# One tile shape, 64 rows by 32 columns, for all products of an attention-and-MLP loop

## The chip, the cores and the metric

The kernel runs on one core of one Trainium2 chip. The metric is the device time of one execution in microseconds. A core has five engines with a queue each: TensorE (PE, whose weight loads are shown apart as PEld), VectorE (DVE), ScalarE (ACT), GpSimd (POOL) and SyncE (SP), which mainly issues DMAs.

## The reference

A block over 2048 tokens of width 640: a layer norm, then attention with 32 heads of 20 channels and an MLP with 1536 hidden channels side by side, both added to the input.

```python
x = A_x
xn = _layernorm(x)
# A: q, k, v = (xn @ wqkv) in 32 heads of Dh = 20
#    o = softmax(q k^T * Dh**-0.5) v ;  out_A = o @ wo
# B: y = _layernorm(xn) ;  h = gelu(y @ w1 + b1) ;  out_B = h @ w2 + b2
return x + _A_ref(xn, A_wqkv, A_wo) + _B_ref(xn, B_w1, B_b1, B_w2, B_b2)
```

Inputs and output are float32. Products are made of float16 or bfloat16 halves, high and low parts, in three passes (`PASS`), or of float32 operands.

## The kernel before, in words

The kernel is one function, `mha_mlp_kernel`, in three stretches. The **first** (lines 155 to 509) loads and normalizes the input, transposes it, splits weights into halves, makes q, k and v, and writes q, k (`qkscr`) and the normalized input (`xscr`) to memory. The w1 weights are loaded by one DMA (line 482) into `w1t`, squared for a scale (line 423) and split in place (line 434).

The **second**, the loop (lines 927 to 964), does the attention, and lays the MLP into it as filling. `ORDER` lists 32 stages: a pair of heads and a half of the queries. A stage has two runs `cc` of 512 queries, and a run goes through 16 blocks of 128 keys. For a block, `scores` (line 578) makes two products, one for each head, of 61 rows by 128 columns, with one head's features in partitions 0 to 60 and the other's in 64 to 124, and issues one exponential on ACT for both (line 586, 128x1024). The score buffers `psS` are three, of two PSUM banks each. Four blocks are a group (`GRP`). In a group the blocks 0 and 1 are "split": their probabilities are used as a bfloat16 upper half and a float16 rest `low`, which DVE makes (`rest`, line 598). Blocks 2 and 3 are "whole" and used as float32.

`pv` (line 603) multiplies a group's probabilities by the values. Its `product` (line 614) takes 128 rows by 32 columns; the four quarters of the PSUM partitions take head 0 and head 1, two sums each, so that one bank holds the output of a run (`psO`, one buffer). Eight products take the upper halves, four the rests, and four the float32 blocks. After a run's last group ACT copies the bank to `ev` (line 636), and after the second run `unload` writes the two partial sums of outputs and denominators to memory (`opart`, `lpart`).

The order of the work is written out by hand. In each group the loop issues scores of two blocks, then the filling, then scores of two blocks, then `pv` of the **previous** group. The filling is a chain of generators: `layer1` (line 777; 1440 passes of 128x128 weights over 256 tokens), `layer2` (line 811; 1152 passes over 320 columns) and, last, the projection with wo. Each step of a generator names its cost in us; the loop gives a credit of `rate` for each group, and takes steps while there is credit, until `CHUNK` is spent or a part has ended (`over`). Parts of both layers share one PSUM bank (`psM`, one buffer). The end of a part starts `gelu` (line 735) or `addup` (line 755) on DVE, which read the bank. `tick`, every two blocks, moves all side work on by one step: stack loads, `gelu`, and `finish` (line 666), which loads the two partial sums back (line 697), adds them (lines 702, 725), divides and writes halves for the projection; it waits a fixed count of ticks for its DMAs. `load_chunk` (line 769) loads 256 tokens of normalized input, two chunks ahead.

The **third** stretch (from line 977) finishes the projection after the loop. A general path behind a flag isn't taken with these inputs.

## Time and profile before

| what | before |
|---|---|
| median of three runs | 1385.02 us (1384.66 to 1385.03) |
| the profiled execution | 1385.2 us |
| its span, first to last instruction | 1383.5 us |
| mean granted TensorE clock | 0.997 |
| PE busy, matmuls | 1350.8 us (98%), 11711 |
| PEld busy, weight loads | 600.9 us (43%), 11711 |
| DVE busy | 1061.7 us (77%) |
| ACT busy | 1126.2 us (81%) |
| POOL busy | 32.9 us (2%) |
| DMA | 125.68 MB, 91 GB/s on the mean |

Busy time counts a product from its start to its modelled end; products overlap, so the time between the starts of two says more than the length of one. In an ordered view a row gives its start, its length, the engine, the line, the operation, output and inputs, rows*columns of the weights, the shape of the moving data, and the count of operations merged in it. In a group's row stand, after the count, its busy time in us and the mean length of one in ns, then the idle time of the engine just ahead of it and what ended that.

### The profile page before, as it was taken

To read this page: it belongs to the slowest core of one execution; us is meant where nothing else is said; L and a number is where in the kernel's file an instruction comes from. 1 tells how busy PE (TensorE), PEld (TensorE's weight loads), DVE (VectorE), ACT (ScalarE), POOL (GpSimd) and SP (SyncE) were. 2 spreads that over 40 slices of the span, in tenths; PEclk is the share of its full clock that TensorE was granted. 3 is DMA by queue.
4 is the path that set the end of the run, shared out by engine and by line. 5 is a ranking of instruction groups with operands and counts; after the bars stand their busy time and mean duration, and the time that the engine had idled before them with its cause. 6 is when DMAs were issued, how large, how long until landed. Compare 5 with 4: busy or idle time off the path is not lost.

```text
span 1383.5 us, 29113 instructions
## 1 busy us (share of the span) xinstructions
PE 1350.8 (98%) x11711; PEld 600.9 (43%) x11711; DVE 1061.7 (77%) x1425; ACT 1126.2 (81%) x1282; POOL 32.9 (2%) x75
## 2 busy tenths in 40 slices
PE   9999999999999999999999999999999999999998
PEld 6555555443333343433343333343334334333375
DVE  6648743899778977889887789877988897888642
ACT  5644323999999999999999999999999999999700
POOL 2000000000000000000000000000000000000000
PEclk9999999999999999999999999999999999999999
DMA  9853413012124231213221123212124322341375
GB/s 265 243 175 109 108 52 110 16 32 64 41 55 111 67 88 34 69 52 102 71 77 33 47 75 103 76 47 58 44 64 113 98 56 70 85 153 59 98 235 179
DMA packets 92320, 125.68 MB, mean 91 GB/s; under 512 B 16905, under 2 KB 58569, under 8 KB 92178
## 3 DMA queue, kind: packets, MB, share of 16 engines
q1 hardware_dynamic: 89218, 117.14, 28.3%
q0 software_dynamic: 2304, 5.24, 2.3%
q8 instruction: 94, 1.54, 0.5%
q10 hardware_dynamic: 656, 1.36, 0.3%
q14 instruction: 48, 0.39, 0.1%
HBM read 80.84 MB, written 42.86 MB: 89 GB/s over the span
## 4 chain that ended last, share of the span: by engine, by line
PE 59%; DVE 11%; ACT 5%; DMA 3%; issue 2%; SPq 1%; DVEq 0%; ACTq 0%
PE o L615 23%; PE s L584 14%; PE py L819 9%; PE pu L787 8%; DVE low L598 5%; PE z L896 5%; ACT p L586 4%; DMA oscr<-oa 1%; DVE u L740 1%; DMA oa<-opart 1%; DVE u L741 1%; DVE w L744 1%; DVE w L745 1%; DVE hT L752 1%; DVE u L750 1%
## 5 line engine op out<-in xcount | busy, mean ns | idle before, releaser
L586 ACT ACTIVATE p<-s 128x1024 f32<-128x1024 f32 x1024 | 973.6, 1042 | 52.4 <-PE s L584 46.2
L598 DVE TENSOR_TENSOR low<-p 128x1024 f16<-128x1024 f32 x512 | 608.8, 1219 | 165.0 <-ACT p L586 164.9
L615 PE MATMUL o<-p,vfull 128*32 128x512 bf16 (+1 forms) x4096 | 433.7, 494 | 0.0
L584 PE MATMUL s<-qs,ks 61*128 61x512 f16 x2048 | 317.7, 382 | 8.7 <-ACT p L586 7.2
L584 PEld LDWEIGHTS <-ks 61*128 61x128 f16 x2048 | 63.9, 94 | 296.4 <-issue 294.2
L787 PE MATMUL pu<-xm,w1t 128*128 128x256 f16 x1440 | 179.2, 274 | 4.1 <-DVE u L740 3.6
L819 PE MATMUL py<-w2t,hT 128*128 128x320 f16 x1152 | 178.6, 301 | 1.7 <-DVE xb L757 1.7
L787 PEld LDWEIGHTS <-w1t 128*128 128x128 f16 x1440 | 130.9, 98 | 71.2 <-issue 57.6
L819 PEld LDWEIGHTS <-hT 128*128 128x128 f16 x1152 | 102.5, 98 | 89.5 <-issue 55.2
L286 PE MATMUL qkp<-xnt,wv 128*128 128x512 f16 x600 | 132.3, 380 | 0.0
L615 PEld LDWEIGHTS <-vfull 128*32 128x32 f16 x3072 | 61.5, 95 | 146.2 <-issue 115.4
L615 PE MATMUL o<-low,vfull 128*32 128x512 f16 x1024 | 107.3, 379 | 6.6 <-DVE low L598 6.4
L300 ACT ACTIVATE qkhl<-qkp,qks 128x1024 f16<-128x1024 f32 (+1 forms) x24 | 23.3, 971 | 84.1 <-PE qkp L286 66.2
L286 PEld LDWEIGHTS <-wv 128*128 128x128 f16 x600 | 58.2, 98 | 67.8
L615 PEld LDWEIGHTS o<-p,vfull 128*32 128x32 f32 x2048 | 63.1, 109 | 50.6 <-issue 0.5
L349 PE MATMUL vp<-wv,xnt 128*128 128x320 f16 x480 | 66.6, 300 | 0.0
L896 PE MATMUL z<-w1t,ot 128*128 128x320 f16 x480 | 65.8, 300 | 0.0
L896 PEld LDWEIGHTS <-ot 128*128 128x128 f16 x480 | 46.7, 98 | 19.8 <-issue 1.7
L349 PEld LDWEIGHTS <-xnt 128*128 128x128 f16 x480 | 46.5, 98 | 18.2
L301 DVE SCALAR_TENSOR_TENSOR qkhl<-qkp,qks,qkhl 128x1024 f16<-128x1024 f32 (+1 forms) x24 | 26.5, 1104 | 34.3 <-ACT qkhl L300 34.3
L857 DVE SCALAR_TENSOR_TENSOR acc<-z,sc,acc 128x320 f32<-128x320 f32 x32 | 17.6, 550 | 45.1 <-PE z L896 42.9
L636 ACT ACTIVATE ev<-o 128x512 f32<-128x512 f32 x64 | 39.4, 615 | 3.3 <-PE o L615 3.3
(168 smaller groups left out, 685.7 us busy)
## 6 DMA issues: line engine op xcount, KB each, us to landing
qkscr<-qkhl SPq DMA_DIRECT2D x40, 256.0 KB
opart<-ev SPq DMA_DIRECT2D x124, 80.0 KB
ks<-qkscr SPq DMA_DIRECT2D x120, 80.0 KB
qs<-qkscr SPq DMA_DIRECT2D x192, 40.0 KB
oa<-opart SPq DMA_DIRECT2D x32, 240.0 KB
xt<-in_A_x_dram SPq DMA_DIRECT2D x16, 320.0 KB
xscr<-xnt SPq DMA_DIRECT2D x4, 1280.0 KB
xm<-xscr SPq DMA_DIRECT2D x8, 640.0 KB
```

The costliest lines, as they stand in the source:

```text
L286: nc.tensor.matmul(ps[:, i, :], wv[:, k, q, a, mm * P : (mm + 1) * P], xnts[c][:, k, b, :], start=(k + n == 0), stop=(k == KD - 1 and n == 2))
L300: nc.scalar.activation(hl[:, 0, i0:i1], ps[:, i0:i1], AF.Copy, scale=a)
L301: nc.vector.scalar_tensor_tensor(hl[:, 1, i0:i1], ps[:, i0:i1], a, hl[:, 0, i0:i1], ALU.mult, ALU.subtract)
L349: nc.tensor.matmul(ps[:, hf, :320], xnts[c][:, k, a, j * P : (j + 1) * P], wv[:, k, 2, b, hf * 320 : (hf + 1) * 320], start=(n == 0), stop ...
L584: nc.tensor.matmul(ps[:, a, :], ks[64 * a : 64 * a + 61, kb * P : (kb + 1) * P], qs[64 * a : 64 * a + 61, cc * 512 : (cc + 1) * 512], star ...
L586: nc.scalar.activation(pt, ps, AF.Exp, scale=QS)
L598: nc.vector.tensor_sub(low, pt, upper(pt))
L615: nc.tensor.matmul(pv.o[32 * q : 32 * q + 32, :], src[:, v0 - PAD * (1 - q % 2) :][:, :32], t, start=q not in pv.begun, stop=last, skip_gr ...
L636: nc.scalar.activation(evs[g, hf][:, cc], pv.o, AF.Copy)
L787: nc.tensor.matmul(ps[:, i], w1v[:, k, (f + i) // 4, a, fo_ : fo_ + P], xnt[:, k, b, :], start=(n == 0), stop=(n == 3 * KD - 1))
L819: nc.tensor.matmul(ps[:, :320], hTs[mc][:, f, a, j * P : (j + 1) * P], w2v[:, f, b, hf * 320 : (hf + 1) * 320], start=(n == 0), stop=(n == ...
L896: nc.tensor.matmul(ps[:, :320], ot[:, k, a, j * P : (j + 1) * P], wov[:, k, b, h * 320 : (h + 1) * 320], start=(n == 0), stop=(n == 3 * KD ...
```

## The change

All products in the loop become products of 64 rows by 32 columns, eight of which cover the array.

- `scores`: eight products of 61x32 for a block in place of two of 61x128.
- `pv`: each product becomes two, one for each half of the rows, into two PSUM banks. ACT copies one bank and DVE adds the other. It is cut in four stages (upper halves, rests, float32, read out), of which each block of the next group issues one.
- `layer1` and `layer2`: each 128x128 pass becomes eight products (`tiles`) into two banks of one tile `mt`, which all parts share. `layer1`'s contraction is laid out anew: `w1` and the normalized input are loaded so that each half of the partitions holds features of its own, and one half of a pass gives hidden channels of its own. `addup` adds two banks with two DVE operations.
- The loop takes the filling at each block but the third of a group; `rate` and `CHUNK` are stated for a block.
- PSUM in the loop: two score buffers in place of three, two banks for the output, two for `mt`.
- `finish`: the second partial sum is added in memory transfer, by a DMA on POOL's queue that accumulates, in place of two DVE adds (the last one keeps them).
- `w1` is loaded by 20 DMAs, a chunk by four plus one, into one buffer and one chunk ahead.

The core of the diff:

```diff
-CHUNK = 1.75
+CHUNK = 0.9
...
+            def load_w1():
+                wt = w1t.rearrange("p k n -> p (k n)").rearrange("p (k j c) -> p k j c", k=2 * KD, c=P)
+                src = w1.rearrange("(k b p) (j r c) -> r b k p j c", b=2, p=64, r=2, c=P)
+                for k in range(2 * KD):
+                    for r in range(2):
+                        nc.sync.dma_start(wt[64 * r : 64 * r + 64, k], src[r, k // KD, k % KD])
...
+            psS = pool(name="psS2", bufs=2, space=PSUM)
+            psO = pool(name="psO2", bufs=1, space=PSUM)
+            psM = pool(name="psM2", bufs=1, space=PSUM)
+            mt = psM.tile([P, 2, 512], F32, tag="m", name="mt")
+
+            def tiles(out, w, t, start, stop, **kw):
+                for r in range(2):
+                    rows = slice(64 * r, 64 * r + 64)
+                    for c in range(0, P, 32):
+                        nc.tensor.matmul(out[c : c + 32, r], w[rows, c : c + 32], t[rows], start=start, stop=stop,
+                                         skip_group_check=True)
...
-                for a in range(2):
-                    nc.tensor.matmul(ps[:, a, :], ks[64 * a : 64 * a + 61, kb * P : (kb + 1) * P],
-                                     qs[64 * a : 64 * a + 61, cc * 512 : (cc + 1) * 512], start=True, stop=True)
+                for c in range(0, P, 32):
+                    for a in range(2):
+                        nc.tensor.matmul(ps[c : c + 32, a, :],
+                                         ks[64 * a : 64 * a + 61, kb * P + c : kb * P + c + 32],
+                                         qs[64 * a : 64 * a + 61, cc * 512 : (cc + 1) * 512], start=True, stop=True)
...
+            def product(unit, q, src, v0, t):
+                kb = unit[3]
+                for r in range(2):
+                    rows = slice(64 * r, 64 * r + 64)
+                    nc.tensor.matmul(pv.o[32 * q : 32 * q + 32, r], src[rows, v0 - PAD * (1 - q % 2) :][:, :32], t[rows],
+                                     start=(q, r) not in pv.begun, stop=kb >= NKB - GRP, skip_group_check=True)
+                    pv.begun.add((q, r))
...
+                elif kb0 == NKB - GRP:
                     if cc == 0:
                         evs[g, hf] = m1.tile([P, 2, 512], F32, tag="ev", name="ev")
-                    nc.scalar.activation(evs[g, hf][:, cc], pv.o, AF.Copy)
+                    nc.scalar.activation(evs[g, hf][:, cc], pv.o[:, 0], AF.Copy)
+                    nc.vector.tensor_add(evs[g, hf][:, cc], pv.o[:, 1], evs[g, hf][:, cc])
...
+                    for cc, kb in ((cc, kb) for cc in range(2) for kb in range(NKB)):
                         units.append([g, hf, cc, kb, scores(g, hf, cc, kb)])
+                        if kb % 2:
+                            tick()
+                        if kb % GRP:
+                            rest(units[-2])
+                        elif prev:
+                            rest(prev[-1])
+                        if prev:
+                            pv(kb % GRP, prev)
+                        credit += rate
+                        spent, over[0] = 0.0, False
+                        while kb % GRP != 2 and credit > 0 and spent < CHUNK and not over[0]:
```

More of the change, by code (lines that the diff above doesn't have):

```diff
@@ L621, in pv @@
+            def pv(stage, units):
+                g, hf, cc, kb0 = units[0][:4]
+                split = [u for u in units if SPLIT[u[3]]]
+                whole = [u for u in units if not SPLIT[u[3]]]
                 of16 = lambda kb, a: 2 * PAD + kb * 2 * VROW + (2 * g + a) * 2 * VW
                 of32 = lambda kb, a: PAD + kb * VROW + (2 * g + a) * VW
-                for kb, up, _ in split:
-                    for a in range(2):
-                        product(2 * a, vhalf, of16(kb, a), up[:, a])
-                        product(2 * a + 1, vhalf, of16(kb, a) + VW, up[:, a])
@@ L695, in finish @@
                     o0, o1, rb = o0[: r1 - r0], o1[: r1 - r0], rb[: r1 - r0]
[L696 to L697 removed]
+                    go(o0, opart[0, r0:r1, cols])
+                    also(o1 if last else o0, opart[1, r0:r1, cols])
                     if c0 == 0:
@@ L836, in mlp @@
                     done[0] = mc == NMC
-                    for i in range(6):
-                        for part in first[i : i + 1] + (second[i - 1 : i] if i else []):
-                            yield from part
+                    for part in first[:2] + second[:1] + first[2:3] + second[1:2] + first[3:] + second[2:]:
+                        yield from part
             pieces = {}
             def load_piece(c):
-                ot = m2.tile([P, KD, 2, MC], F16, tag="xnt", name="ot")
+                if c == 0:
+                    pieces["ot"] = m1.tile([P, 2 * KD, 2, MC], F16, tag="xnt", name="ot")
+                ot = pieces["ot"][:, c % 2 * KD : (c % 2 + 1) * KD]
                 acc = m0.tile([P, KF, 2, MC], F16, tag="hT", name="acc")
@@ L977, in mha_mlp_kernel @@
                 more(2)
-                pv(prev)
+                for stage in range(4):
+                    pv(stage, prev)
                 while more(1):
```

186 lines of the change are left out of this document (90 added, 96 removed).

## The prediction

> **What bounds the kernel now.** I read the profile in this order: busy time by stage, the groups, the order of time on ScalarE, the order of time on TensorE, then the chain and the waits for what hangs on DMAs. The view by stage (columns: us, then busy time and count of PE, PEld, DVE, ACT, POOL, then clock, DMA share, GB/s) cuts the span before, in and behind the attention loop:
>
> ```profile
> 0.00:256.00 256.00, 250.02 (x1612) 140.44 (x1612) 153.99 (x327) 125.92 (x159) 16.99 (x57) 0.99 0.49 143
> 256.00:1310.00 1054.00, 1034.06 (x9598) 412.15 (x9597) 884.33 (x1054) 999.97 (x1124) 15.92 (x18) 1.00 0.25 70
> 1310.00:1383.50 73.50, 66.75 (x505) 48.28 (x503) 23.39 (x45) 0.28 (x1) 0.00 (x0) 0.98 0.69 211
> ```
>
> In the loop two engines are nearly full: PE 1034 of 1054 us and ACT 1000. The change touches little but the loop, so what matters is how much of PE's 1034 is not arithmetic, and that ACT leaves only 54 us to be won. ACT in order of time and three groups:
>
> ```profile
> 698.31 7.61 ACT L586 ACTIVATE p<-s 128x1024 f32<-128x1024 f32 x8 [0.19 <-PE s L584]
> 705.77 0.63 ACT L636 ACTIVATE ev<-o 128x512 f32<-128x512 f32 x1
> 706.25 3.96 ACT L586 ACTIVATE p<-s 128x1024 f32<-128x1024 f32 x4
> ```
> ```profile
> L586 ACT ACTIVATE p<-s 128x1024 f32<-128x1024 f32 x1024 | 973.6, 1042 | 52.4 <-PE s L584 46.2
> L598 DVE TENSOR_TENSOR low<-p 128x1024 f16<-128x1024 f32 x512 | 608.8, 1219 | 165.0 <-ACT p L586 164.9
> L787 PE MATMUL pu<-xm,w1t 128*128 128x256 f16 x1440 | 179.2, 274 | 4.1 <-DVE u L740 3.6
> L819 PE MATMUL py<-w2t,hT 128*128 128x320 f16 x1152 | 178.6, 301 | 1.7 <-DVE xb L757 1.7
> ```
>
> Eight exponentials take 705.77 - 698.31 = 7.46 us, 0.93 each, and the copy of the output 706.25 - 705.77 = 0.48 before the next may start. ACT idles 46.2 us for scores. Now PE, through one group of four key blocks, and one stretch of the second layer:
>
> ```profile
> 699.73 0.38 PE L584 MATMUL s<-qs,ks 61*128 61x512 f16 x2
> 700.04 0.64 PE L615 MATMUL o<-p,vfull 128*32 128x512 bf16 x8
> 700.50 0.39 PE L615 MATMUL o<-low,vfull 128*32 128x512 f16 x4
> 700.72 1.03 PE L615 MATMUL o<-p,vfull 128*32 128x512 f32 x8
> 701.68 0.60 PE L584 MATMUL s<-qs,ks 61*128 61x512 f16 x4
> 702.22 1.16 PE L787 MATMUL pu<-xm,w1t 128*128 128x256 f16 x9
> 703.31 0.61 PE L584 MATMUL s<-qs,ks 61*128 61x512 f16 x4
> 703.84 0.64 PE L615 MATMUL o<-p,vfull 128*32 128x512 bf16 x8
> ```
> ```profile
> 1181.59 1.80 PE L819 MATMUL py<-w2t,hT 128*128 128x320 f16 x12
> ```
>
> A second pair of scores starts 0.60 - 0.38 = 0.22 us behind the first, but the first product of another shape 700.04 - 699.73 = 0.31 behind: the change of shape costs 0.09. First-layer passes come every (1.16 - 0.274)/8 = 0.111 us, the last starts at 703.11, and scores at 703.31: 0.20 - 0.11 = 0.09 again. Four such changes stand in a group of 4.11 us: 0.37 x 256 groups = 95 us. That is what one shape can save on PE.
>
> **The change part by part.**
>
> *Shape.* The array work stays: eight 64x32 products fill the array as one 128x128, four 128x32 or two 61x128 did. Per group PE then needs 4 x 0.22 for scores, 3 x 0.22 for the half-width products, 2 x 0.43 for the float32 ones ((1.03 - 0.593) is the second round's start; 0.593 us is the mean in the row below), 2.40 in all, and the layers (1440 x 0.111 + 1152 x 0.136)/256 = 1.24, with 0.136 = (1.80 - 0.301)/11. Sum 3.64, over the loop 932 us against 1054. PE would stop being the bound; ACT is late next.
>
> ```profile
> L615 PE MATMUL o<-p,vfull 128*32 128x512 f32 x2048 | 269.7, 593 | 0.0
> ```
>
> *Four to eight times as many instructions.* Scores 1024 x 8, half-width products 3072 x 2, float32 2048 x 2, layers (1440 + 1152) x 8: 39,168 pairs of load and product where 9,598 stand. No row shows a long run of such small pairs. The nearest, product bursts and loads:
>
> ```profile
> 34.03 0.38 PE L286 MATMUL qkp<-xnt,wv 128*128 128x512 f16 x1
> 34.34 0.29 PE L321 MATMUL norms<-sq,heads 128*32 128x128 bf16 x8
> 34.57 0.39 PE L286 MATMUL qkp<-xnt,wv 128*128 128x512 f16 x1
> ```
> ```profile
> L615 PEld LDWEIGHTS <-vfull 128*32 128x32 f16 x3072 | 61.5, 95 | 146.2 <-issue 115.4
> L321 PE MATMUL norms<-sq,heads 128*32 128x128 bf16 x160 | 5.9, 224 | 0.5 <-DVE sq L306 0.5
> ```
> ```profile
> 700.03 0.35 PEld L615 LDWEIGHTS <-vfull 128*32 128x32 f16 x12 [0.42 <-issue]
> ```
>
> Eight norm products of 0.22 us are over in 0.29, so their starts lie within 0.07: 0.01 a pair, from a burst that had been waiting. Twelve loads of 0.095 take 0.35, so up to (0.35 - 0.095)/11 = 0.023 a pair (those were held back by the products between). A pass of eight pairs thus lies between its array time and 0.185 us. I take the array time, being nearer to the burst; the upper end is a rival.
> [...]
>
> *The output bank, and where the new wait is.* The bank of the attention output has one buffer, before and after. Before, its copy was issued at the end of a group and the next product of that bank came a group later. After, the stages are spread over the blocks: float32 products at block 2, the copy on ACT and a new add on DVE behind block 3's exponential, and the first product of the next 16 blocks at block 4. Let block 2's exponential end at 0 with ACT full. Block 3's runs to 0.93, the copy starts there and is done at 0.93 + 0.63 = 1.56, the add (the row of the same size below, 0.69) at 2.25, and PE may go on at about 2.3. PE had issued block 4's scores at about 0.4. Behind the waiting product stand its own second round (0.44 in all), one step of the layers (3 x 0.111 = 0.33) and block 5's scores, which end about 0.22 + 0.17 later: 3.5. ACT has finished block 4 at 0.93 + 0.48 + 0.93 = 2.34: it idles about 1.2 us, 64 times in the loop, 77 us. Only 54 us were there to be won. Bounds: 0.4 a time (PE far ahead, no layer step, a faster add), 2.0 (two steps, and a 1.22 us `low` ahead of the add).
>
> ```profile
> L741 DVE TENSOR_TENSOR u<-u,b1t 128x512 f32<-128x512 f32 x48 | 33.2, 692 | 1.7
> L757 DVE SCALAR_TENSOR_TENSOR xb<-py,sc,xb 128x320 f32<-128x320 f32 x32 | 17.4, 545 | 0.0
> L725 DVE TENSOR_TENSOR oa<-oa 120x512 f32<-120x512 f32 x16 | 11.0, 686 | 2.7 <-DMA rb<-linv 1.5 <-DMA oa<-opart 1.2
> ```
>
> *DVE.* 64 adds x 0.69 = 44 and 32 second `addup` x 0.545 = 17 come, the adds of `finish` (about 15) go: 884 to some 930 us. It fits beside ACT, so I cost it at nothing beyond the wait above.
>
> *The layers' bank* has one buffer. About 52 times a part follows that needs what the part before still has read out: PE end + 0.2 + one or two DVE operations, while the next block's scores and products cover 0.4 to 1.3; some 0.44 us on the mean, 23 us of PE. With the bank of the output (PE waits 2.3 - 0.6 = 1.7 x 64 = 109) PE comes to 932 + 109 + 23 = 1064, still under ACT's total below. The third score buffer is gone too; its cover is part of the walk above.
>
> *Queues.* Partial sums are now added by a DMA on POOL's queue behind the first load, not beside it:
>
> ```profile
> 433.03 2.49 DMA oscr<-oa
> 435.52 0.02 issue
> ...
> 435.97 6.91 DMA oa<-opart
> ```
> ```profile
> DMA to landing us min/median/max: 4.1/4.4/8.9
> ```
>
> The second is the landing of the adding DMAs that exist (`xb`, same queue; they wait behind the new ones, but have a whole layer part of time). In a second half: 2.5 + 2.5 to 6.9 + 4.4 = 9.4 to 13.8 us against four ticks of two blocks, about 8.2. DVE may wait 1 to 5 us, 11 times, with `low` queued behind it. `low` is used three blocks or more after it is made, which covers most: I take 5 us, bounds 0 and 40. The chunk load is four DMAs into one buffer, issued after a chunk's last first-layer part; two second-layer parts (9.8 us of fill, over 30 us of loop) hide it, and 4.0 of held credit in the first chunk.
>
> *w1's load* becomes 20 DMAs of 512-byte runs:
>
> ```profile
> L482 SPq DMA_DIRECT2D w1t<-in_B_w_dram x1: 380/380/380, 55.8 to 55.8; - x1
> ```
> ```profile
> 73.16 1.48 ACT L423 ACTIVATE junk<-w1t 128x1536 bf16<-128x1536 f32 x1 [0.44 <-DMA w1t<-in_B_w_dram]
> ```
>
> SP issues for 19 x 0.38 = 7 us more, ahead of the next stores and input loads, and the reader already waits 0.44 us. ACT is half idle there, PE is not: I take 2 us, bounds 0 and 8.
>
> *Sum.* Loop: ACT's 1000 + 77 + 5 = 1082 in place of 1054. Span 1383.5 + 28 + 2 = 1413.5; the profiled execution was 1385.2 us, 1.7 over its span and 0.2 over the median of the three runs. Forecast: 1415 us.
>
> **The rivals.**
>
> *The bank's wait is covered, so the change is faster.* If ACT loses at most 0.4 us at each boundary, the loop is 1000 + 26 + 5 = 1031 at most and the time 1364; with nothing lost and 1000 alone, 1333. I price it at 1350. It decides in one place: the first product after each sixteenth block must find its bank read out within about 0.9 us of PE asking. For it: 95 us of shape changes are real, and PE keeps 3.64 of work in a group in which ACT needs 3.9. Against: nothing in the order of issue shortens exponential, copy, add. 0.27.
>
> *Small pairs are the bound.* At 0.185 us a pass the layers take 10.125 x 0.185 = 1.87 a group, PE 4.27 x 256 + 109 = 1202, the time 1202 + 329.5 + 2 + 1.7 = 1535 (329.5 is the span outside the loop). From (1082 - 109)/256 - 2.40 = 1.40 a group, 0.138 us a pass or 17 ns a pair, PE decides. For it: 23 ns is the only rate that a row shows over more than eight. 0.12.
>
> *The shape isn't what costs 0.09.* If the gap comes with any change of operand, PE is 95 worse, 1159, and the time 1492. Against: the norms above start 0.31 us behind a product of another shape that streams like the scores, and scores behind scores 0.22. 0.05.
>
> *Gains and waits cancel* within 0.2%: 0.06. The forecast, 1388 to 1450: 0.50.
>
> **How the numbers follow.** 0.2% is about what a measurement of this kernel can tell from no change. Faster 0.27; same 0.06; slower 0.50 + 0.12 + 0.05 = 0.67. The range runs from 1345, near the faster rival's low end, to 1500, past the third rival and short of the second's 1535; about 0.15 is left out. The likeliest case alone is 1388 to 1450.
>
> **What would show each step.** One shape: no 0.09 gaps between scores, products and layers, PE's busy time in the loop still high but its sum of passes lower. The wait: PE's products waiting for the DVE add, some 64 times at 1 to 2 us, and ACT's exponentials idle for scores by far more than 46 us. Small pairs: first-layer passes of eight further apart than 0.111 us, with the loads or "issue" ahead of them and ACT idle everywhere, not at every sixteenth block. Wrong I would be above all if that product hardly waits; then ACT is back to back and the loop ends near 1020 us.

## The result and the profile after

| | before | after |
|---|---|---|
| median | 1385.03 us (1384.66 to 1385.12, 4 runs) | 1589.49 us (1588.76 to 1592.52, 4 runs) |
| ratio, 95% interval | 1 | 1.1481 [1.1461, 1.1501] |
| profiled execution, its span | 1385.2, 1383.5 us | 1592.52, 1590.8 us |
| mean granted clock | 0.997 | 0.976 |
| first to last product of scores | 232.5 to 1305.0: 1072.5 us | 236.1 to 1502.1: 1266.0 us |
| behind the last scores | 78.5 us | 88.7 us |

The changed kernel is 14.8% slower: 174 us above the forecast and outside its range. Of the 207 us between the spans the loop has 193.5, the stretch ahead of it 3.6, the stretch behind it 10.

From the page of the changed kernel, busy time by engine, and in its part on DMA queues the larger of the two of kind "instruction":

```profile
PE 1356.9 (85%) x41119; PEld 861.7 (54%) x41119; DVE 1116.7 (70%) x1488; ACT 1146.9 (72%) x1282; POOL 61.5 (4%) x108
...
q8 instruction: 323, 5.29, 1.4%
```

The same queue before:

```profile
q8 instruction: 94, 1.54, 0.5%
```

PE runs 41,119 products and as many loads for 11,711 each, and the queue's packets rise with them: 41,119 / 323 = 127 pairs of load and product for a packet, and 11,711 / 94 = 125 before. A packet is 5.29 MB / 323 = 16.4 KB. In the loop alone, from 236.1 to 1502.1 us, the trace has this many of them:

```profile
q8 instruction: 306, 5.01, 1.6%
```

That is 1266.0 / 306 = 4.1 us from one to the next, and 39,168 / 306 = 128 pairs of load and product for each. The view by stage of the changed kernel, two stretches in the middle of the loop:

```profile
300.00:800.00 500.00, 414.05 (x15384) 267.06 (x15372) 375.50 (x435) 409.11 (x449) 15.69 (x18) 0.97 0.27 64
800.00:1300.00 500.00, 417.31 (x15708) 269.36 (x15693) 374.99 (x441) 411.77 (x451) 18.16 (x21) 0.98 0.28 67
```

No engine is full any more: PE is busy 83% of the time and ACT 82%, where they had 98% and 95%. Each waits for the other or for something else. The groups of the changed kernel (after the bar, idle time just ahead of the group and what ended it) say for what:

```profile
L614 ACT ACTIVATE p<-s 128x1024 f32<-128x1024 f32 x1024 | 993.7, 1030 | 225.6 <-PE s L611 212.3 <-PE o L636 5.2 <-DVE oa L770 1.2
L611 PE MATMUL s<-qs,ks 61*32 61x512 f16 x8192 | 501.0, 385 | 27.9 <-issue 17.9 <-ACT p L614 8.1
L636 PE MATMUL o<-p,vfull 64*32 64x512 bf16 (+1 forms) x8192 | 489.0, 499 | 114.9 <-DVE ev L671 107.5 <-issue 6.9
L542 PE MATMUL mt<-w2t,hT 64*32 64x320 f16 x9216 | 266.2, 302 | 14.3 <-DVE xb L797 6.7 <-issue 3.4 <-DVE u L779 3.0
L542 PE MATMUL mt<-xm,w1t 64*32 64x256 f16 x11520 | 263.9, 272 | 45.4 <-issue 25.0 <-DVE xb L797 12.8 <-DVE u L779 5.0
L671 DVE TENSOR_TENSOR ev<-o,ev 128x512 f32<-128x512 f32 x64 | 44.1, 689 | 52.5 <-ACT ev L670 51.3
```
```profile
ACT p L614 <- PE s L611: 212.3, 226, 4.5
...
PE o L636 <- DVE ev L671: 107.5, 63, 3.4
```

ACT idles 212.3 us for scores where it idled 46.2, and it does so 226 times (view of waits: total, times, longest), not only at the 64 read-outs of the output. PE waits 63 times for the read-out, 107.5 us, and some 53 us with "issue" as the reason: for nothing that a semaphore shows. One such place, PE in order of time:

```profile
763.65 1.06 PE L636 MATMUL o<-p,vfull 64*32 64x512 f32 x16
764.51 0.70 PE L611 MATMUL s<-qs,ks 61*32 61x512 f16 x8
764.83 1.06 PE L542 MATMUL mt<-w2t,hT 64*32 64x320 f16 x44
...
767.60 0.39 PE L611 MATMUL s<-qs,ks 61*32 61x512 f16 x2
771.85 0.62 PE L611 MATMUL s<-qs,ks 61*32 61x512 f16 x4 [3.86 <-issue]
771.87 2.31 PE L636 MATMUL o<-p,vfull 64*32 64x512 f32 x16
```

The eight score products of one block are torn: four have started by 767.60, then nothing for almost 4 us, then the other four. The trace shows no semaphore that holds up the second four, and the times of the packets in queue q8 point to the instructions themselves: one lands at 763.25, the next begins only at 768.95, more than a microsecond after the last of the first four has started, and lands at 770.39; the other four scores start 1.46 us later. ACT lost 3.65 us there. Behind the gap the float32 stage takes 2.31 us instead of 1.06: the granted clock (the third figure from the end) is halved, 0.50. The view by stage in the gap and behind it:

```profile
768.00:771.80 3.80, 0.00 (x0) 0.00 (x0) 3.62 (x5) 0.87 (x2) 0.00 (x0) 0.77 0.95 209
773.00:776.00 3.00, 3.00 (x60) 1.65 (x45) 0.00 (x0) 1.89 (x3) 0.00 (x0) 0.50 0.02 7
```

The length of a wait alone does not tell whether the clock is halved behind it: in nomlp, a run below, the same stage takes 0.65 us behind one wait of 1.72 us and 0.99 behind another, where the clock is at 0.50, as its order of time on PE and its view by stage show:

```profile
708.11 0.65 PE L634 MATMUL o<-p,vfull 64*32 64x512 bf16 x16 [1.72 <-DVE ev L669]
...
724.22 0.99 PE L634 MATMUL o<-p,vfull 64*32 64x512 bf16 x16 [1.72 <-DVE ev L669]
```
```profile
724.40:727.70 3.30, 3.30 (x56) 1.36 (x48) 2.11 (x2) 1.94 (x2) 0.00 (x0) 0.50 0.31 83
```

From the mean clock of the two stretches of the changed kernel, 0.97 and 0.98, I estimate that some 50 of their 1000 us ran at half clock.

### The profile page after: what moved, and what is told of

Same layout as the page of the kernel before. It is cut to its first block, busy times and chain, and to the rows that moved or that the text cites. A ratio compares the mean times of both kernels' runs of the same rounds, so it can differ in the third digit from the quotient of the medians.

```text
span 1590.8 us, 88461 instructions
## 1 busy us (share of the span) xinstructions
PE 1356.9 (85%) x41119; PEld 861.7 (54%) x41119; DVE 1116.7 (70%) x1488; ACT 1146.9 (72%) x1282; POOL 61.5 (4%) x108
## 3 DMA queue, kind: packets, MB, share of 16 engines
q1 hardware_dynamic: 103314, 117.22, 27.3%
q8 instruction: 323, 5.29, 1.4%
## 4 chain that ended last, share of the span: by engine, by line
PE 52%; DVE 18%; ACT 10%; DMA 9%; issue 8%; SPq 1%; ACTq 0%; POOL 0%; DVEq 0%; POOLq 0%
PE o L636 16%; PE mt L542 13%; PE s L611 10%; ACT p L614 7%; DVE low L626 7%; PE qkp L290 6%; PE z L939 4%; PE vp L353 3%; DVE ev L671 3%; DMA oa<-opart 2%; ACT ev L670 2%; DVE xb L797 2%; DVE u L779 2%; DMA xt<-in_A_x_dram 1%; DMA qkscr<-qkhl 1%
## 5 line engine op out<-in xcount | busy, mean ns | idle before, releaser
L614 ACT ACTIVATE p<-s 128x1024 f32<-128x1024 f32 x1024 | 993.7, 1030 | 225.6 <-PE s L611 212.3
L636 PE MATMUL o<-p,vfull 64*32 64x512 bf16 (+1 forms) x8192 | 489.0, 499 | 114.9 <-DVE ev L671 107.5
L611 PE MATMUL s<-qs,ks 61*32 61x512 f16 x8192 | 501.0, 385 | 27.9 <-issue 17.9
L542 PE MATMUL mt<-xm,w1t 64*32 64x256 f16 x11520 | 263.9, 272 | 45.4 <-issue 25.0
L542 PE MATMUL mt<-w2t,hT 64*32 64x320 f16 x9216 | 266.2, 302 | 14.3 <-DVE xb L797 6.7
L611 PEld LDWEIGHTS <-ks 61*32 61x32 f16 x8192 | 187.4, 93 | 163.5 <-issue 136.6
L542 PEld LDWEIGHTS <-w1t 64*32 64x32 f16 x11520 | 194.2, 93 | 130.2 <-issue 85.2
L542 PEld LDWEIGHTS <-hT 64*32 64x32 f16 x9216 | 169.4, 94 | 92.5 <-issue 44.2
L636 PEld LDWEIGHTS <-vfull 64*32 64x32 f16 x6144 | 117.1, 94 | 180.9 <-issue 166.1
L636 PE MATMUL o<-low,vfull 64*32 64x512 f16 x2048 | 129.9, 390 | 11.5 <-DVE low L626 8.6
L636 PEld LDWEIGHTS o<-p,vfull 64*32 64x32 f32 x4096 | 99.3, 109 | 21.5 <-issue 15.6
```

Of the source, the lines that this page charges most:

```text
L542: nc.tensor.matmul(out[c : c + 32, r], w[rows, c : c + 32], t[rows], start=start, stop=stop, skip_group_check=True)
L611: nc.tensor.matmul(ps[c : c + 32, a, :], ks[64 * a : 64 * a + 61, kb * P + c : kb * P + c + 32], qs[64 * a : 64 * a + 61, cc * 512 : (cc + ...
L614: nc.scalar.activation(pt, ps, AF.Exp, scale=QS)
L636: nc.tensor.matmul(pv.o[32 * q : 32 * q + 32, r], src[rows, v0 - PAD * (1 - q % 2) :][:, :32], t[rows], start=(q, r) not in pv.begun, stop ...
```

## The experiments

Two theories stood against each other at first. **Supply:** with four times as many products in the loop, instructions come too slowly for PE. **New waits:** what the prediction had in its sum, the single bank of the output in the block-by-block order, costs more than forecast, and the count of products costs nothing. A third, the lost score buffer, came up with the runs. In the table the ratio is to the kernel before on the same chip, and the loop goes from the first to the last product of scores in the profiled run.

| run | us | ratio [95%] | loop us |
|---|---|---|---|
| mb_supply | 662.07 | - | - |
| thin | 1596.38 | 1.1471 [1.1268, 1.1673] | 1263.1 |
| nomlp | 1435.28 | 1.0346 [1.0316, 1.0376] | 1111.6 |
| nomlp_s3 | 1434.65 | 1.0341 [1.0285, 1.0398] | 1111.1 |
| nomlp_o2 | 1352.18 | 0.9747 [0.9719, 0.9775] | 1029.3 |
| few_layers | 1497.88 | 1.0812 [1.0790, 1.0833] | 1164.2 |
| few_evac | 1471.58 | 1.0622 [1.0584, 1.0660] | 1141.9 |
| evac_early | 1568.57 | 1.1337 [1.1312, 1.1362] | 1242.1 |
| two_pass | 1537.64 | 1.1096 [1.1071, 1.1121] | 1206.3 |
| scores_small | 1391.98 | 1.0058 [1.0039, 1.0077] | 1079.2 |
| layers_full | 1580.04 | 1.1434 [1.1395, 1.1473] | 1259.3 |
| finish_before | 1604.17 | 1.1569 [1.1525, 1.1613] | 1275.1 |
| order_before | 1551.17 | 1.1187 [1.1166, 1.1207] | 1234.5 |
| hybrid | 1461.22 | 1.0550 [1.0533, 1.0568] | 1143.0 |
| hybrid_blocks | 1483.12 | 1.0697 [1.0679, 1.0715] | 1168.2 |
| before_2buf | 1481.11 | 1.0683 [1.0663, 1.0703] | 1164.5 |

### The supply of instructions

**mb_supply** is not this kernel: long runs of one kind of product and nothing else on the core. Its core:

```diff
+        def small256(n):
+            for _ in range(n):
+                for r in range(2):
+                    for c in range(0, P, 32):
+                        nc.tensor.matmul(pc[c : c + 32, r, :256], w[64 * r : 64 * r + 64, c : c + 32],
+                                         t[64 * r : 64 * r + 64, :256], start=True, stop=True)
...
+        small512(500)
...
+        small320(500)
...
+        small256(500)
```

> This kernel computes nothing of the reference: it sends long runs of independent products to PE, with no other engine and no DMA beside them. Theory S (supply): PE's instructions arrive 256 at a time, every 3.4 to 3.5 us at best, as the fetches in the changed kernel's trace do; that is 13.5 ns an instruction, 27 ns for a load and its product. Then a pass of eight 64x32 products takes 0.216 us at 512, at 320 and at 256 columns alike, after a first stretch at the array's rate: 500 passes about 108 us in each of the three runs. Theory N (the array's rate holds, the loss is all in waits): 0.216, 0.136 and 0.109 us a pass, so 108, 68 and 55 us. [...] Passes of 128x128 take 0.109 in all. In the last run, eight small products of 512 columns and one 128x128 of 256 take turns: 0.216 + 0.107 + two changes of shape at 0.09 = 0.50 us a turn if the shape is what costs, 0.33 if it is not.

The views of three lines of it (count, lengths in ns, first and last start in us), for 512, 320 and 256 columns:

```profile
L36 PE MATMUL pa<-t,w x4000: 372/376/387, 63.4 to 176.2; 64*32 64x512 f16 x191
```
```profile
L43 PE MATMUL pb<-t,w x4000: 292/296/308, 220.3 to 332.6; 64*32 64x320 f16 x191
```
```profile
L50 PE MATMUL pc<-t,w x4000: 266/269/418, 376.6 to 488.3; 64*32 64x256 f16 x191
```

4000 pairs take 112.8, 112.3 and 111.7 us: 28 ns a pair in all three. For 512 columns this is the rate of the products themselves (376 of them stand without a wait in 10.61 us, (10.61 - 0.38) / 375 = 27.3 ns each), and PE's idle time with "issue" as the reason is 1.4 us there; for 320 and 256 columns it is 38.4 and 48.5 us. So it is these two that show a limit other than the products' own rate. In order of time the last of them is no even row:

```profile
406.90 2.06 PE L50 MATMUL pc<-t,w 64*32 64x256 f16 x128 [0.69 <-issue]
410.65 1.94 PE L50 MATMUL pc<-t,w 64*32 64x256 f16 x128 [1.68 <-issue]
414.12 1.94 PE L50 MATMUL pc<-t,w 64*32 64x256 f16 x128 [1.53 <-issue]
```

128 pairs run at (1.94 - 0.27) / 127 = 13 ns each, eight of them in 0.105 us where a 128x128 pass of the layers took 0.111, and then PE waits until 3.5 to 3.75 us after the start of the last 128. 128 is also the count of pairs for a packet in the changed kernel's loop: 256 instructions in 16.4 KB, 64 bytes each. The rows agree with a packet of 128 pairs every 3.5 to 3.75 us; the times of this run's packets are not shown. Of the layers' passes as they were before, 0.111 us each, 128 held 14 us of work; of the small ones 128 hold 1.8. The expectation of the supply theory was met; at 512 columns the theory of the array's rate expected the same 108 us.

The last run of mb_supply, eight small products of 512 columns and one of 128x128 in turn, prices the change of shape:

```profile
532.27 0.41 PE L61 MATMUL pa<-t,w 64*32 64x512 f16 x8
532.61 0.28 PE L63 MATMUL pc<-t,w 128*128 128x256 f16 x1
532.83 0.41 PE L61 MATMUL pa<-t,w 64*32 64x512 f16 x8
```

Each turn takes 0.55 to 0.56 us, above the 0.50 that was expected if the shape costs and far above the 0.33 if it does not. With the 0.218 us that eight small products took alone (8 x 27.3 ns) and 0.111 for the 128x128 pass, (0.555 - 0.218 - 0.111) / 2 = 0.113 us a change on the mean.

**thin** keeps all instructions of the changed kernel and takes three quarters of the layers' columns away:

```diff
+                        cut = MC if n == 0 else 64
-                        tiles(out, w1v[:, sl // 3, sl % 3, a, c0 : c0 + P], xnt[:, k, b, :],
+                        tiles(out[:, :, :cut], w1v[:, sl // 3, sl % 3, a, c0 : c0 + P], xnt[:, k, b, :cut],
...
+                        cut = 320 if n == 0 else 64
-                        tiles(mt[:, :, :320], hTs[mc][:, f, a, j * P : (j + 1) * P],
-                              w2v[:, f, b, hf * 320 : (hf + 1) * 320], start=(n == 0), stop=(n == 3 * KF - 1))
+                        tiles(mt[:, :, :cut], hTs[mc][:, f, a, j * P : (j + 1) * P],
+                              w2v[:, f, b, hf * 320 : hf * 320 + cut], start=(n == 0), stop=(n == 3 * KF - 1))
```

> The changed kernel with all passes of the layers but the first of each sum cut to 64 columns (the MLP's part of the output is incomplete): the layers keep all of their 20,736 pairs of load and product, but their array time falls from 315 to some 85 us. If the supply of instructions decides (28 ns a pair, whatever its columns): about the changed kernel's time, 1560 to 1590. If the array's own time does: near the kernel without the layers, 1435 to 1470.

The loop is 1263.1 us for 1266.0: three quarters of the layers' columns gone, and nothing gained. The time, 1596, is 6 us above the range of the supply theory and far from the other's 1470. From its order of time on PE, a block's score products torn again:

```profile
762.32 0.78 PE L542 MATMUL mt<-w2t,hT 64*32 64x64 f16 x48
...
764.95 0.39 PE L611 MATMUL s<-qs,ks 61*32 61x512 f16 x2
769.34 0.61 PE L611 MATMUL s<-qs,ks 61*32 61x512 f16 x4 [4.00 <-issue]
```

48 pairs pass in 0.78 us, and PE then waits so much longer. For the layers' products the count of instructions decides in this run, not their columns.

**two_pass** leaves the third pass of halves (`a == 1`) out of both layers, 6,912 pairs:

```diff
+                        if a == 0:
                             tiles(out, w1v[:, sl // 3, sl % 3, a, c0 : c0 + P], xnt[:, k, b, :],
```

> The changed kernel without the third pass (low weights by high data) of both layers: a third of the MLP's products is left out, order, credit and all waits stay. Array time falls by (1440 x 0.109 + 1152 x 0.136) / 3 = 104 us; the loop's pairs fall from 39,168 to 32,256, 903 us at 28 ns a pair. Theory S: most of the 100 us in which PE stood without instructions goes as well: 1390 to 1430 us. Theory N (no loss to supply): 1589 - 104 = 1485 us.

At 1537.64 us it is 52 us faster than the changed kernel, far from what either theory gave. PE's idle time for "issue" ahead of scores and both layers falls from 46 to 11 us, but its wait for the read-out rises to 131.7:

```profile
L636 PE MATMUL o<-p,vfull 64*32 64x512 bf16 (+1 forms) x8192 | 472.9, 508 | 132.1 <-DVE ev L671 131.7 <-issue 0.3
L611 PE MATMUL s<-qs,ks 61*32 61x512 f16 x8192 | 465.8, 392 | 34.1 <-ACT p L614 20.2 <-issue 7.0
```

Where the supply gives way, the wait for the bank takes part of the gain. That without the loss of supply the forecast would come true was too simple: the two losses stand in for each other.

### The bank of the output, the score buffers and the layers

**nomlp** leaves the MLP's products and the arithmetic of `gelu` and `addup` out of the changed kernel, and with them its demand for instructions. **nomlp_s3** and **nomlp_o2** spend the free PSUM:

```diff
-                        tiles(out, w1v[:, sl // 3, sl % 3, a, c0 : c0 + P], xnt[:, k, b, :],
-                              start=(n == 0), stop=(n == 6 * KD - 1))
...
-            psS = pool(name="psS2", bufs=2, space=PSUM)
+            psS = pool(name="psS2", bufs=3, space=PSUM)
...
-            psO = pool(name="psO2", bufs=1, space=PSUM)
+            psO = pool(name="psO2", bufs=2, space=PSUM)
```

> The changed kernel's block-by-block order, with the MLP's products and the gelu and addup arithmetic left out (the MLP's part of the output is missing), so that TensorE has only scores, products with the values and the projection: 20,480 fewer small pairs. In the loop TensorE then needs about 2.4 us a group of ScalarE's 3.9, so neither its work nor the supply of instructions can decide. Output-bank theory: ScalarE idles 0.8 to 1.2 us at each of the 64 boundaries; loop about 985 + 50 to 77, time 1365 to 1395. Score-buffer theory: with two score buffers and nothing ahead of the scores on TensorE, ScalarE is fed and idles only where the order holds the scores back; 1330 to 1360.

> As nomlp (MLP's arithmetic left out), with three score buffers in place of two. Output-bank theory: a third buffer lets one more exponential stand ready at each boundary, 0.9 us, so that 40 to 60 us of nomlp's idle time on ScalarE go. If instead the idle time comes from products that wait for low or for instructions: same as nomlp within 10 us.

> As nomlp (MLP's arithmetic left out), with two buffers of the output's banks in place of one, so that no product waits for the copy and the add. Output-bank theory: all 50 to 77 us of the boundary's idle time on ScalarE go, and the loop falls to about 985 to 1000. Score-buffer theory: within 10 us of nomlp, and only nomlp_s3 is shorter.

ACT of nomlp in order of time through one read-out, and then of nomlp_o2:

```profile
706.69 0.65 ACT L668 ACTIVATE ev<-o 128x512 f32<-128x512 f32 x1
707.16 1.08 ACT L612 ACTIVATE p<-s 128x1024 f32<-128x1024 f32 x1
709.10 13.86 ACT L612 ACTIVATE p<-s 128x1024 f32<-128x1024 f32 x15 [0.85 <-PE s L609]
722.79 0.66 ACT L668 ACTIVATE ev<-o 128x512 f32<-128x512 f32 x1
```
```profile
703.91 0.71 ACT L668 ACTIVATE ev<-o 128x512 f32<-128x512 f32 x1
704.39 14.90 ACT L612 ACTIVATE p<-s 128x1024 f32<-128x1024 f32 x16
719.07 0.71 ACT L668 ACTIVATE ev<-o 128x512 f32<-128x512 f32 x1
```

With one buffer ACT idles behind the first exponential of each run; with two it works through all sixteen. The second buffer takes 82.3 us off the loop, 1.3 at each of 64 read-outs; the third score buffer takes 0.5. So in this order the wait for the bank counts and the score buffer doesn't. The 82.3 hold a share of halved clock, which I did not separate: PE idles more in nomlp, and its mean clock is 0.935 for 0.978 in nomlp_o2. Two sizes were missed. nomlp is 40 us above the range of the output-bank theory, and nomlp_o2's loop 29 above its 1000; and that theory too expected 40 to 60 us from the third score buffer, which gave none.

**few_layers** keeps everything but makes only the first pass of each sum of the layers, 640 of 20,736 pairs; **few_evac** is the same with the read-out one block earlier, as in **evac_early**:

```diff
-                        tiles(out, w1v[:, sl // 3, sl % 3, a, c0 : c0 + P], xnt[:, k, b, :],
-                              start=(n == 0), stop=(n == 6 * KD - 1))
+                        if n == 0:
+                            tiles(out, w1v[:, sl // 3, sl % 3, a, c0 : c0 + P], xnt[:, k, b, :], start=True, stop=True)
...
-                elif kb0 == NKB - GRP:
+                if stage == 2 and kb0 == NKB - GRP:
```

> The changed kernel without most of the MLP's arithmetic: of the 30 passes of a first-layer part and the 36 of a second-layer part one is left. Everything else, the order and the credit too, stays. 19,072 pairs, 534 us of supply: no wait for instructions, and PE is half idle. It prices the output bank's wait alone: by the walk of the prediction, without a layer step, ACT idles 3.15 - 2.34 = 0.8 us at each of 64 boundaries: 1000 + 51 in the loop, about 1385 us. If the wait costs ACT nothing when PE has time, 1335 us.

> As the run before it, without most of the MLP's arithmetic, and with the copy and the add of the output bank right behind the float32 products. By the same walk the bank is free 1.35 us after block 2's exponential, and block 5's scores are ready at 2.2, ahead of the end of block 4's exponential at 2.34: ACT never idles, 1335 us, about 50 less than the run with the late copy. If the boundary isn't what made ACT idle, the two runs are equal.

> The changed kernel, with the copy and the add of the output bank issued right behind the float32 products (block 2) and not behind block 3's exponential. The first product of the next run then waits about 0.8 us for the bank where it waits 1.7 now, 64 times. Theory N (the waits are the loss): 60 us less, 1530 us. Theory S: while PE waits, instructions go on arriving, so a shorter wait is partly paid back by waiting for instructions: 20 to 40 us less, 1550 to 1570.

few_layers has neither the array's work nor the instructions of the layers, and its loop is still 52.6 us longer than nomlp's. Some 28 us of this are no wait: ACT's own part of `gelu`, 48 operations (the last row below), raises its busy time in the loop from 986.1 to 1014.6 us. The rest are `gelu` and `addup` on DVE and the waits for their bank:

```profile
L636 PE MATMUL o<-p,vfull 64*32 64x512 bf16 (+1 forms) x8192 | 478.9, 521 | 141.5 <-DVE ev L671 141.5
...
L542 PE MATMUL mt<-xm,w1t 64*32 64x256 f16 x384 | 15.7, 293 | 20.0 <-DVE xb L797 10.4 <-DVE u L779 8.1 <-DMA xm<-xscr 1.1
...
L542 PE MATMUL mt<-w2t,hT 64*32 64x320 f16 x256 | 10.9, 312 | 21.2 <-DVE xb L797 12.7 <-DVE u L779 8.3
```
```profile
L787 ACT ACTIVATE w<-w 128x512 f32<-128x512 f32 x48 | 31.2, 650 | 0.0
```

The wait for the read-out grows from 119.7 us in nomlp to 141.5, with DVE's new work in the same queue, and 39 us of waits for the layers' bank come. The earlier read-out cuts PE's wait for the bank from 107.5 to 52.3 us in evac_early (141.5 to 80.0 in few_evac) and the loop by 24 (22). The 21 us of evac_early are what the supply theory expected of it. few_layers and few_evac lie 113 and 137 us above the 1385 and 1335 that I had expected: with the supply out of the way their loops still take 1164.2 and 1141.9 us, in which ACT is idle 150 and 129. So the supply is not the only cause. How much of this idle time is the waits for the two banks and how much the lower clock that comes with them (0.95 on the mean) is not separated.

### One part of the change at a time

**scores_small** is the kernel before with the eight small score products and nothing else:

```diff
-                for a in range(2):
-                    nc.tensor.matmul(ps[:, a, :], ks[64 * a : 64 * a + 61, kb * P : (kb + 1) * P],
+                for c in range(0, P, 32):
+                    for a in range(2):
+                        nc.tensor.matmul(ps[c : c + 32, a, :],
```

> The kernel before, with one part of the change alone: the scores of a block are eight products of 61x32 in place of two of 61x128. All else, the number of changes of shape too, stays. Theory S: 9,598 + 6,144 pairs in the loop are 31,500 instructions, 425 us at 13.5 ns, far below the loop's 1054, so nothing waits for instructions: 1385 us within 1%. [...] If small products cost anything by themselves, 1024 blocks show it: 1400 or more.

0.6% slower, within the 1% that the supply theory allowed. 6,144 more pairs cost 7 us where the average need stays below the supply: 13,336 in the 900 us from 300 to 1200, 67 ns each.

**finish_before** takes the accumulating DMAs back:

```diff
-                    also(o1 if last else o0, opart[1, r0:r1, cols])
+                    for p, o in enumerate((o0, o1)):
+                        go(o, opart[p, r0:r1, cols])
...
-                    if last:
-                        nc.vector.tensor_add(o0, o0, o1)
+                    nc.vector.tensor_add(o0, o0, o1)
```

> The changed kernel with the partial sums added by DVE again, as before the change, and loaded side by side on SP's queue, in place of the accumulating DMAs on POOL's. In the changed kernel DVE stood 25 us in all before operations on these sums. If that wait passes on to PE one for one: 25 less and 15 us of DVE adds more, 1565 to 1580 us. If it is absorbed, 1589 within 0.5%.

Its ratio is 1.1569 for the changed kernel's 1.1481, some 12 us more, where I had expected a gain or nothing. So that part of the change is a small gain. The run moves the loads to SP's queue together with the adds, so that it is the adds on DVE that cost is likely, not shown.

**layers_full** is the changed kernel with the layers in 128x128 passes as before:

```diff
-                        tiles(out, w1v[:, sl // 3, sl % 3, a, c0 : c0 + P], xnt[:, k, b, :],
-                              start=(n == 0), stop=(n == 6 * KD - 1))
+                            nc.tensor.matmul(ps[:, i], w1v[:, k, (f + i) // 4, a, fo_ : fo_ + P], xnt[:, k, b, :],
+                                             start=(n == 0), stop=(n == 3 * KD - 1))
```

> The changed kernel with both layers as before the change: passes of 128x128, one bank for their sums, w1 loaded by one DMA; attention stays in 64x32, with the same staged order and the same wait for the output bank. 18,432 + 2,592 pairs in the loop are 42,000 instructions, 570 us at 13.5 ns. Theory S: no wait for instructions and no halved clock are left; 768 fillings bring two changes of shape each, 0.09 apiece, 143 us of PE: 932 + 143 + 109 + 23 = 1207 in the loop, 1538 us in all. Theory N (the loss of the changed kernel is in waits that this one has too): 1589 + 143, about 1730 us.

18,144 pairs fewer, no score product waits for "issue" any more, and it is still only 9 us faster, between the two theories' 1538 and 1730. The price is in its order of time:

```profile
704.32 0.40 PE L593 MATMUL s<-qs,ks 61*32 61x512 f16 x8
704.65 0.83 PE L808 MATMUL pu<-xm,w1t 128*128 128x256 f16 x6
705.41 0.41 PE L593 MATMUL s<-qs,ks 61*32 61x512 f16 x8
705.64 0.63 PE L618 MATMUL o<-p,vfull 64*32 64x512 bf16 x16
```

Eight score products stream 0.22 us, but the layers start 0.33 behind: 0.11 for the change of shape. The last layer pass starts at 704.65 + 0.83 - 0.28 = 705.20, streams 0.11, and scores start at 705.41: 0.10. The products behind these scores have other operands and the same shape, and start 0.23 later: next to nothing. Six changes of shape in a group, up to 1536 in the loop, are some 160 us.

**order_before** has all products small but the order of the loop, `CHUNK` and buffers in SBUF of before (scores of two blocks, filling, scores of two blocks, all of `pv`). **hybrid** is that with 128x128 layers, **hybrid_blocks** a block-by-block order of it that takes the filling once a group, issues no `pv` behind a group's first scores, and has the old adds in `finish`, and **before_2buf** is the kernel before with two score buffers in the loop:

```diff
-                        while kb % GRP != 2 and credit > 0 and spent < CHUNK and not over[0]:
+                        if kb % GRP == 1:
...
+                            if prev:
+                                for stage in range(4):
+                                    pv(stage, prev)
```
```diff
-        tc.tile_pool(name="psS", bufs=3, space=PSUM) as psS,
...
+            psS = pool(name="psS2", bufs=2, space=PSUM)
```

> The changed kernel, all products in 64x32, but with the loop's order from before the change, one filling a group and the four stages in one go, so that the output bank has a group's time to be read out. No change of shape and no wait for that bank are left. Theory S: 39,168 pairs at 28 ns are 1097 us of supply for a loop in which ACT needs 1000, so the loop takes at least 1097 and, since supply can't be stored through the float32 stretches, some 50 to 100 more: 1470 to 1540 us. Theory N (the bank's wait and what follows from it were the loss): PE's 932 and ACT's 1000 us, 1345 to 1365 us.

> Attention in 64x32 products, both layers in 128x128, and the order of the loop as before the change: scores of two blocks, one filling, scores of two blocks, then the four stages of the previous group's products in one go; two buffers for the layers' bank. Two changes of shape are left in a group, and the output bank has a group's time to be read out. Theory S (supply, plus the bank's wait): 21,024 pairs are 590 us at 28 ns, so nothing waits for instructions; PE needs 2.40 + 1.24 + 0.2 = 3.84 us a group, 983 us, and ACT's 1000 is the bound again: 1345 to 1365 us, faster than before. Rival R (the half-row products of attention themselves are slower on the chip than 128-row ones): 1400 or more, as in the run with full layers.

> Attention in 64x32, layers in 128x128, and an order made for two score buffers: each block issues its scores alone; block 0 of a group takes the filling, block 1 the upper halves and the rests of the previous group, block 2 its float32 products, block 3 reads out. Two changes of shape a group, three blocks between the bank's read-out and its next use. PE needs 3.84 us a group, 983 in the loop, 21,024 pairs 590 us of supply. Theory S with the two waits removed: ACT is the bound again, 1345 to 1375 us. If a filling of 1.4 us in one block starves ACT with two buffers, 1400 to 1430.

> The kernel before, with two score buffers in the loop in place of three, nothing else. In the two runs that kept the old order of the loop with small attention products, PE waited some 170 us for ACT to give back a score buffer. If it is the third buffer that is missing there: 1430 to 1460 us. If those waits come from the products' shape, 1385 to 1395.

In order_before, 1551, the wait for the output's bank is gone (PE waits 3.4 us for the read-out), and 1345 to 1365 would have followed if that wait were the main loss; it lies 11 us above the range of the supply theory. hybrid and hybrid_blocks, expected near 1360, came out 100 and more above it. hybrid's 1461 is also what the rival in its expectation gave, half-row products that are slower by themselves; but before_2buf, whose products have the old shapes, is as slow, 21 us above what I had expected of it. It says why: in the order of before a score buffer is worth much. Without the third, before's own loop grows from 1072.5 to 1164.5 us, because PE waits for ACT to free a buffer and ACT then for scores. The group of exponentials and that of scores in before_2buf:

```profile
L593 ACT ACTIVATE p<-s 128x1024 f32<-128x1024 f32 x1024 | 982.8, 1026 | 118.2 <-PE s L591 113.1
...
L591 PE MATMUL s<-qs,ks 61*128 61x512 f16 x2048 | 351.7, 383 | 78.4 <-ACT p L593 74.7
```

hybrid (1143.0) keeps this loss, and so does order_before: of the 162 us that its loop is longer than before's, some 92 may be the missing buffer, so that it does not tell supply and buffer apart alone. order_before against hybrid, both with two score buffers, sets the small layers apart: 18,144 more pairs cost 91.5 us of loop, although hybrid still changes shape twice a group and order_before never does. hybrid also has a second buffer for the layers' bank, but PE waits only 3.3 + 2.8 = 6 us for the one of order_before. No version that computes the whole reference beats the kernel before.

## Why the prediction was wrong, point by point

**Small pairs: the step that failed.** "I take the array time, being nearer to the burst." For one pass that is right: in the changed kernel 44 pairs of the second layer take (1.06 - 0.30) / 43 = 18 ns each, 0.14 us a pass for 0.136 forecast. It is wrong for a long run, which the burst did not bound: mb_supply took 28 ns a pair, sustained, with 128 pairs every 3.5 to 3.75 us. At that price the loop's 39,168 pairs take 39,168 x 0.028 = 1097 us, more than ACT's 1000 and the 932 that the sum gave PE. The rival with small pairs as the bound had the right point ("from 17 ns a pair, PE decides"), the right sign in the profile (ACT idle everywhere, 226 times) and the nearest price, 1535 for 1589; its rate, 23 ns from a row of loads, was not the right cause, since in mb_supply such pairs run at 13 ns for 128 of them before PE waits. I gave it 0.12.

**What it cost, as a ladder of loops.** nomlp_o2 1029.3; one buffer for the output 1111.6 (+82.3); `gelu`, `addup` and the bank of the layers, few_layers 1164.2 (+52.6, some 28 of them ACT's own work, which the forecast's 1000 holds); the other 20,096 pairs at 64 columns, thin 1263.1 (+98.9); their full columns 1266.0 (+2.9). The order in which parts are put back decides what each seems to cost: they share the same idle time.

**The wait for the output's bank: right.** Forecast 1.7 us x 64 = 109 on PE and 77 on ACT; PE waits 107.5 in 63 times, and the second buffer gives 82.3 us back where neither layers nor supply bind. That 107.5 comes so near to 109 is partly luck: where PE is not held back by the supply, the same wait is 119.7 us (nomlp) and 141.5 us (few_layers). The rival in which the wait is covered is excluded.

**The sum took the larger of two engines.** "PE comes to 932 + 109 + 23 = 1064, still under ACT's total below." Waits on PE do not vanish under ACT's total: they can delay the next scores. few_layers has hardly any of the layers' products, and its loop of 1164.2 us is still 82 above the forecast's 1082: ACT is busy 1014.6 us and idle 149.6, where the sum had 77 + 5 over ACT's 1000. This is the second step that failed: 82 us here, against the 102 (1266.0 - 1164.2) that the other pairs of the layers add. The bank of the layers itself was sized about right, 28 us of PE in the changed kernel (12.8 + 5.0 + 6.7 + 3.0) for 23. Likewise "I cost it at nothing beyond the wait above" for DVE is doubtful: in finish_before the old adds, about 15 us of DVE, put 12 us on the time together with the loads' other queue.

**The third score buffer.** "Its cover is part of the walk above" is right in the changed order (nomlp_s3: 0.5 us). In the order of before it would have cost 92.

**The change of shape: right.** Forecast 0.09 us each, measured 0.10 to 0.11. (Four times 0.09 is 0.36 us a group, 92 us in the loop, for the 95 that were named.) The saving is real, but the free time that it made on PE went into waiting, for instructions and for the banks. The rival in which it isn't the shape that costs is excluded.

**Queues and w1.** DVE waits for the accumulated sums about as forecast, 17.1 us in 9 waits where 11 of 1 to 5 were named; finish_before shows the exchange to be a gain:

```profile
L766 DVE TENSOR_TENSOR oa<-oa,rb 120x512 f32<-120x512 f32 (+2 forms) x23 | 16.3, 710 | 23.5 <-DMA oa<-opart 17.1 <-DMA accscr<-xb 4.4 <-DMA opart<-ev 2.0
```

The stretch ahead of the loop grew by 3.6 us for 2. The 10 us behind the loop were not forecast.

**What stays open.** In the changed kernel the supply, 1097 us by mb_supply's price, and PE's waits for the two banks, `low` and ACT, 107.5 + 27.5 + 8.6 + 8.1, sum to 1249 of 1266: that would fit a supply that stops while PE waits. The same sum for order_before misses 35 of 1234.5. So it is argued from sums, not shown, that supply and waits add up. How much of each loss is halved clock was not separated.

## What to carry to other kernels

Count instructions as a resource: pairs of load and product times the sustained price of a pair (28 ns in mb_supply, 1097 us for this loop), against the time of the bound engine (1000 us of ACT), and distrust a rate that comes from a burst of eight (0.01 us a pair here). The single read-out buffer cost PE most of its walk of exponential, copy and add in this order, which asks for the bank a block later: 107.5 us in 63 waits, 1.7 each. Do not hide waits of one engine under the total of another when the two feed each other: in few_layers that left out 82 us.

## What the runs showed of the hardware

- In mb_supply 4000 pairs of load and product took 28 ns each with 320 and with 256 columns. With 256 columns 128 pairs ran at 13 ns each, and the next 128 started 3.5 to 3.75 us after them. The loop of the changed kernel took one packet of 16.4 KB for 128 pairs, 306 for 39,168.
- Sets of products without any wait between them are torn, by 3.86 us in the changed kernel and by 4.00 us in thin. In the first the packet began only 1.35 us after the last product ahead of the gap had started, and the products went on 1.46 us after it had landed; for the second the times of the packets are not shown.
- The clock was halved, 0.50, behind that first gap, where the float32 stage took 2.31 us for 1.06, and in nomlp behind one wait of 1.72 us but not behind another, where the same stage took 0.65 us for 0.99.
- A change between 64x32 and 128x128 products cost 0.10 and 0.11 us in the rows of layers_full, and 0.11 us on the mean in mb_supply.
